# Decode attention in two layers on one core: layer 1's softmax in two passes of four heads

## Chip, cores and metric

One core of one Trainium2 chip. The metric is the device time of one execution in microseconds; lower is better. Times shown here are of the kernel before the change.

## The reference, cut to what matters

Four blocks run one after the other on x (8 sequences of one token, 448 features): attention A, MLP B, then the same A and the same B again. The second pass over A reads the same caches and weights.

```
def _A_ref(x, k_cache, v_cache, wq, wo):
    W = min(4096, max(256, Sk // 4))              # 1024 of 4096 positions
    q = (x @ wq).reshape(B, Sq, 16, 256)          # 16 query heads on 8 KV heads
    k, v = the last W positions of the caches, each KV head used twice
    p = softmax(einsum("bhqd,bhkd->bhqk", q, k) * 256 ** -0.5)
    return einsum("bhqk,bhkd->bhqd", p, v).reshape(B, Sq, 4096) @ wo
def _B_ref(x, w1, w2):
    return silu(x @ w1) @ w2                      # 448 -> 1792 -> 448
x = x + _A_ref(layernorm(x), ...); x = x + _B_ref(layernorm(x), ...)      # layer 1
x = x + _A_ref(layernorm(x), ...); x = x + _B_ref(layernorm(x), ...)      # layer 2
```

All arrays are bfloat16. The window of K and of V is 4 MB for each sequence, 64 MB in all, and the weights are some 12 MB; each of them is read from HBM once.

## The kernel before

**Loads.** A slot holds 1 MB: two KV heads' window of K, or of V. A batch (one sequence) has four K loads and four V loads, in the order K0 to K3, V0 to V3. There are 15 slots in a ring, so load n goes into the place of load n - 15. Since both layers use the same K and V, a K slot is free only when layer 2's scores of its batch are done, and a V slot when layer 2's products are. All these loads stand in the queue of SyncE in their order (`load_kv`, L511) and wait there for the slot.

**One batch.** VectorE turns K in its slot by 32 x 32 blocks (`transposes`, L655; in the names KW for the whole half slot, 1024 wide, KT for 512 wide). TensorE makes the scores (`scores`, L672), named S*layer*.*half*: half 0 is KV heads 0 to 3 from K0 and K1, half 1 heads 4 to 7 from K2 and K3. Half 0 writes 32 rows of each 32-row group, half 1 then writes the first 16 of them, so that one bank of 128 x 256 holds all heads. `softmax` then goes over that bank: maximum on VectorE (L687, max), scaling on ScalarE (L692, mq), a matmul that spreads it (L695, mx), a reduction (L698, mb), the exponential on ScalarE (L699, exp), a permuting matmul (L701, perm), a transpose on VectorE (L703, turn), the sums (L705) and their reciprocal (L708, rl). `products` multiplies with V (L715, PV0 for layer 1, PV1 for layer 2), one V slot at a time. For layer 1 the last V slot's products are separate (`products_late`, L726, in `late`), 256 wide. `o_turn` evicts (L739), turns the output into columns with matmuls (L743) and copies them (L747); `wo_rows` multiplies with wo (L768, wo0 for the first 24 rows and wo7 for the 8 rows of the last V slot). `fold` evicts (L774) and adds the row into x as columns (L544, L547).

`chain` is what follows in the same batch: x masked (L779, xb1), statistics (L785, L788, L790 on GpSimd), w1 in halves (L559) with a turn on VectorE each (L564), tanh (L812) and product (L814), w2 (L826), a second fold, xb2 (L779), statistics, the queries of layer 2 in halves (L841, wq0 and wq1; turns L846; products L847, qm0 and qm1; L854, qx0 and qx1; copies on ScalarE, L858, qbd0 and qbd1). Then come layer 2's scores (S1.0 and S1.1), its softmax and its products.

The queries of layer 1 for all batches are made at the start; `q_blocks1` spreads those of one batch over `qbd[0]` on GpSimd (L641). For the last batch layer 2 has a softmax of its own in two parts; layer 2's MLP runs once for batches 0 to 6 (`final_rows`) and once for batch 7 (`final_last`). `warm` issues matmuls with zero weights (L795, fill) into waits.

**Staging.** In the program order, `chain(b)` and layer 2's attention of batch b stand beside layer 1's attention of batch b + 1:

```
    for b in range(NB):
        chain(b)
        if b < LAST:
            q_blocks1(b + 1)
            attend1(b + 1, 0)
```

This order only makes the dependencies. The order in which each engine really issues its work is written out by hand in `ORDER`, a list of task numbers for TensorE, VectorE, ScalarE and GpSimd; `emit` puts a semaphore wait before a task where another engine's result is needed. Each engine is in order, so a task that waits holds up all that stands behind it on its engine.

**Room.** `qbd[0]` holds layer 1's queries of the current batch: half 0 in columns 16 to 271, half 1 in 272 to 527. `e_sb[0]` and `pT_sb[0]` (exponentials and their transpose) are the same two pieces: `PT[0] = QB(0, 0)`, `EK[0] = QB(0, 1)`.

Of the kernel before, what the change touches and what calls it, by code (L numbers as in the profile page):

```python
# [36 lines left out]
    "dve":  # L37
# [14 lines left out]
    "act":  # L52
# [8 lines left out]
    "pool":  # L61
        "0 1 86 123 124 231 261 262 248 388 357 387 374 522 492 523 509 648 647 617 634 772 773 742 759 867 897 898 "
        "884 1023 1022 992 1009 1110 1127 1154 1217",
}

# [158 lines left out]
def bass_interleave_layers__sliding_block_cached__dense_activation_silu__decode_kernel(  # L224
# [18 lines left out]
    R = 15  # L243
    NP = HKV // 2
    WIDE = (0, 1)
    LATE = 2
    SLOT = 4096
    WARM = (8, 12, 5, 4, 4, 4, 4, 4, 3)
    XC = 5
# [66 lines left out]
    def bk(i):  # L316
        return [("bank", i)]
# [694 lines left out]
    def values1(b):  # L1012
# [9 lines left out]
        for j in range(NP - 1):  # L1022
            products(b, 0, j, OB[0])
# [93 lines left out]
```

## Time and profile before

| what | value |
|---|---|
| three runs | 238.09, 238.39, 242.27 us; median 238.39 |
| the profiled execution | 236.37 us, of which 234.6 us span from the first to the last instruction |
| mean granted TensorE clock | 0.992 |
| PE busy | 175.4 us (75%) |
| DVE busy | 156.9 us (67%), of it K transposes (L655) 79.6 |
| ACT busy | 70.7 us (30%) |
| POOL busy | 22.7 us (10%) |
| moved by DMA | 78.22 MB, mean 333 GB/s |
| chain that ended last | PE 34%, DMA 28%, DVE 25%, ACT 6% |

PE is TensorE's matmuls, DVE is VectorE, ACT ScalarE, POOL GpSimd. A share of busy time is an average over stretches with different limits, so the stretches have to be read one by one. "L655" is line 655 of the kernel before. The chain is followed back from the last instruction to what released it each time.

### The profile page before, as it was taken

The numbers are of one execution on the slowest core, as the hardware profiler recorded it, in microseconds if no ns is written. First come the engines' busy times: TensorE is split into PE (matmuls) and PEld (weight loads), VectorE is DVE, ScalarE is ACT, GpSimd is POOL, SyncE is SP. The second block draws the span as 40 slices with busy tenths as digits, with TensorE's granted clock in tenths as the row PEclk, the third lists the DMA queues.
The fourth block names the chain that finished last, engine by engine and source line by source line (L and its number), as shares of the span: only waits on it lengthen the run. The fifth ranks groups of instructions, "written<-read, shape, count | busy, mean of one in ns | idle before, by whom it ended". The sixth has DMA issues, their size and how long they took to land.

```text
span 234.6 us, 8630 instructions
## 1 busy us (share of the span) xinstructions
PE 175.4 (75%) x3885; PEld 99.1 (42%) x3885; DVE 156.9 (67%) x389; ACT 70.7 (30%) x219; POOL 22.7 (10%) x41
## 2 busy tenths in 40 slices
PE   0021554498878998879859888889898879899994
PEld 0011431134454465356426544455455436554652
DVE  6329899987965794598379739865893588304623
ACT  2000190622222412341333143232422422253332
POOL 1000220002001100120021011000200200001020
PEclk9999999999999999999999999999999979999999
DMA  6999999999999998997999799989987997500000
GB/s 176 422 423 407 380 381 420 412 426 419 418 419 423 395 401 334 426 423 291 383 422 422 292 418 422 419 321 415 423 362 295 419 420 312 183 3 3 3 3 4
DMA packets 13610, 78.22 MB, mean 333 GB/s; under 512 B 1271, under 2 KB 4294, under 8 KB 5126
## 3 DMA queue, kind: packets, MB, share of 16 engines
q1 hardware_dynamic: 13414, 77.32, 81.6%
q8 instruction: 30, 0.49, 0.8%
q10 hardware_dynamic: 160, 0.36, 0.5%
q14 instruction: 6, 0.05, 0.1%
HBM read 77.67 MB, written 0.01 MB: 331 GB/s over the span
## 4 chain that ended last, share of the span: by engine, by line
PE 34%; DMA 28%; DVE 25%; ACT 6%; SPq 2%; issue 2%; POOL 1%; DVEq 0%; ACTq 0%
DMA slot<-in_A_k_cache_dram 28%; DVE slot L655 13%; PE bank L672 9%; DVE slot L482 4%; PE bank L854 4%; PE bank L715 3%; PE pair L841 3%; PE pair L768 3%; PE bank L841 3%; ACT qbd L858 2%; PE pair L826 1%; ACT ot L774 1%; PE bank L785 1%; DVE bank L687 1%; PE pair L544 1%
## 5 line engine op out<-in xcount | busy, mean ns | idle before, releaser
L655 DVE STREAM_TRANSPOSE slot<-slot 128x512 uint32<-128x512 uint32 (+1 forms) x96 | 79.6, 865 | 18.1 <-DMA slot<-in_A_k_cache_dram 17.5
L672 PE MATMUL bank<-slot,qbd 128*32 128x256 bf16 (+1 forms) x1024 | 39.4, 288 | 6.6 <-ACT qbd L858 2.6
L672 PEld LDWEIGHTS bank<-slot,qbd 128*32 128x32 bf16 (+1 forms) x1024 | 26.8, 94 | 15.5 <-ACT qbd L858 5.6
L715 PE MATMUL bank<-slot,qbd 128*24 128x512 bf16 (+3 forms) x416 | 30.6, 394 | 1.1 <-DVE qbd L703 1.0
L795 PE MATMUL bank<-wq_sb,cols 128*1 128x512 bf16 x192 | 19.5, 420 | 10.1 <-DMA wq_sb<-in_A_wq_dram 10.1
L790 POOL TENSOR_TENSOR fcols<-fcols 128x1 f32<-128x1 f32 x17 | 9.4, 552 | 108.0 <-ACT fcols L788 81.8
L739 ACT ACTIVATE ot<-bank,q1s 128x512 bf16<-128x512 f32 (+1 forms) x16 | 10.8, 672 | 26.2 <-DVE q1s L708 10.8
L768 PE MATMUL pair<-wo_sb,q1s 128*1 128x449 bf16 x288 | 15.8, 353 | 0.3 <-ACT q1s L747 0.3
L641 POOL TENSOR_TENSOR qbd<-q1s,fcols 128x256 bf16<-128x256 bf16 x16 | 9.6, 612 | 65.8 <-PE bank L743 39.9
L858 ACT ACTIVATE qbd<-bank 128x256 bf16<-128x256 f32 x16 | 6.1, 383 | 29.7 <-PE bank L854 29.7
L687 DVE CUSTOM_DVE_ANT_1 bank<-bank,fcols 128x256 f32<-128x256 f32 x17 | 7.3, 432 | 10.2 <-PE bank L672 9.4
L715 PEld LDWEIGHTS bank<-slot,qbd 128*24 128x24 bf16 (+3 forms) x416 | 9.5, 93 | 9.6 <-issue 2.4
L692 ACT ACTIVATE fcols<-fcols,q1s 128x16 f32<-128x16 f32 x15 | 4.6, 310 | 24.3 <-DVE q1s L687 19.6
L482 DVE TENSOR_REDUCE slot<-wo_sb 128x6 f32<-128x2688 bf16 x4 | 11.7, 2928 | 0.0
L708 DVE RECIPROCAL q1s<-bank 128x1 f32<-128x1 f32 x17 | 2.8, 162 | 12.6 <-PE bank L705 12.6
L703 DVE STREAM_TRANSPOSE qbd<-bank 128x256 bf16<-128x256 bf16 x17 | 7.9, 467 | 4.3 <-PE bank L701 4.3
L490 ACT ACTIVATE slot<-w_sb 128x448 bf16<-128x448 bf16 x6 | 3.5, 576 | 22.9 <-DMA w_sb<-in_B_w_dram 22.8
L779 DVE TENSOR_TENSOR q1s<-pair,fcols 128x5 bf16<-128x5 f32 x17 | 2.5, 145 | 11.2 <-PE pair L547 11.1
L854 PE MATMUL bank<-qbd,band 128*128 128x64 bf16 x64 | 9.8, 286 | 0.2 <-DVE qbd L847 0.2
L785 PE MATMUL bank<-q1s 128*128 128x1 bf16 x68 | 4.3, 167 | 7.4 <-DVE q1s L779 7.4
L795 PEld LDWEIGHTS bank<-wq_sb,cols 128*1 128x1 bf16 x192 | 4.4, 84 | 12.0 <-issue 10.4
L695 PE MATMUL bank<-fcols,quad 128*32 128x8 f32 x136 | 4.3, 188 | 6.3 <-ACT fcols L692 6.0
(165 smaller groups left out, 265.4 us busy)
## 6 DMA issues: line engine op xcount, KB each, us to landing
slot<-in_A_k_cache_dram SPq DMA_DIRECT2D x32, 1024.0 KB, 10.9
slot<-in_A_v_cache_dram SPq DMA_DIRECT2D x31, 1024.0 KB, 10.8
wo_sb<-in_A_wo_dram SPq DMA_DIRECT2D x4, 896.0 KB, 15.2
wq_sb<-in_A_wq_dram SPq DMA_DIRECT2D x3, 1024.0 KB, 7.9
w_sb<-in_B_w_dram SPq DMA_DIRECT2D x1, 1568.0 KB, 21.8
w_sb<-in_B_w_dram SPq DMA_DIRECT2D x1, 1344.0 KB, 19.3
slot<-in_A_v_cache_dram SPq DMA_DIRECT2D x2, 512.0 KB, 4.8
wq_sb<-in_A_wq_dram ACTq DMA_DIRECT2D x1, 256.0 KB, 3.5
```

Of the source, the lines that this page charges most:

```text
L482: dve(lambda e, rows=rows, s=s: e.tensor_reduce(s, rows[:, :, R0:M1].rearrange("p c (a n) -> p c a n", a=2), AX.X, ALU.add, negate=True), ...
L641: pool(lambda e, k2=k2: e.tensor_tensor(qdata(0, k2), q1s[:, b, 64 * k2:64 * k2 + 64].rearrange("p (n r) -> p n r", r=2).unsqueeze(3) .bro ...
L655: dve(lambda e, v=v: e.transpose(v, v), keys, keys, 0.15 + (i1 - i0) * 512 / 950, b, ("KW%d" if i1 - i0 > 1 else "KT%d") % (2 * j + h))
L672: fns.append(lambda e, w=w, j=j, kv=kv, cb=cb, par=par: e.matmul(sc[32 * j:32 * j + up_to, 0:256], w, kv, start=(cb == 0 and par == 0), st ...
L687: dve(lambda e: e.tensor_tensor_reduce(x.rearrange("p (c h) -> p c h", h=2), x.rearrange("p (c h) -> p c h", h=2), parity.unsqueeze(1).bro ...
L715: pe([lambda e, t=t, h=h: e.matmul(bank[ob][32 * t:32 * t + m, :], pT_sb[L][:, 64 * t + 32 * h:64 * t + 32 * h + m], v[:, 2048 * h + 512 * ...
L739: act(lambda e: e.activation(o_t, src[1], ACTF.Copy, scale=sm[b][:, 4 * L + 3:4 * L + 4]), bk(src[0]) + [("sm", b, L, 3)], okey, 0.62, b, ...
L768: fns.append(lambda e, i=i, w=w, c0=c0: e.matmul(bank[XB][32 * (i % 4):32 * (i % 4) + 1, c0:c0 + D + 1], oT[:, oT_col(i):oT_col(i) + 1], w ...
L795: pe([lambda e, i=i: e.matmul(bank[OB[0]][32 * i:32 * i + 1, :], zero_b, wq_sb[:, 512 * i:512 * i + 512], start=True, stop=True, tile_posi ...
L841: pe([lambda e, j=j, c=c, qh=qh, k2=k2, h=h, n=n: e.matmul(qh[32 * j:32 * j + 1, :], xbt[b][:, xcol(c, k2):xcol(c, k2) + 1], view(wq_sb[:] ...
L854: pe([lambda e, qs=qs, k2=k2, q=q: e.matmul(qs[:, q:256:4], band[:, 96 - 32 * q:224 - 32 * q], view(qm[k2], 0, [(32, 2), (1, 8), (8, 4)]), ...
L858: act(lambda e, qs=qs, k2=k2: e.activation(qbd[1][:, 16 + 256 * k2:272 + 256 * k2], qs, ACTF.Copy), bk(lb), QB(1, k2) + QM * k2, 0.42, b, ...
```

## The change

Layer 1's softmax runs twice for each batch. The pass g = 0 runs after the first half of the scores (heads 0 to 3) and the pass g = 1 after the second half; each goes over the whole bank of 128 x 256, and only the rows of its own half are used. The exponentials of pass g, and then their transpose, lie where the queries of half g were (`eb = pb`), as do the scaled maxima (`m4`). The pass g = 0 uses layer 1's output bank for its small matmuls, the pass g = 1 the bank used before.

The second half's scores go into the same bank as the first half's, so they now wait until the exponential of pass 0 has read it.

The products of V0 and V1 use pass 0 and stay 512 wide. The products of V2 and V3 use pass 1 and are both made 256 wide in `late` (`LATE` is 4 where it was 2), so wo has 16 rows after the first part (wo0) and 16 after the late part (wo7).

The four lists in `ORDER` are new. TensorE's matmuls are 136 more, nine a batch for the extra pass and eight a batch for the halved products; VectorE gets 32 operations more and ScalarE 16. The loads and their order are as before. In the new lists layer 1's products and output rows mostly stand ahead of layer 2's products, xb1 stands ahead of the transposes of the next batch's second K slot or just behind the first one's, and of the final rows of batches 0 to 6 most stand behind layer 2's scores of batch 7.

```diff
-    LATE = 2
+    LATE = 4
...
-    def softmax(b, L, part=None):
+    def softmax(b, L, part=None, g=0):
 
         sb, n, m = (SC[L], L, L) if part is None else (part[0], part[1], 1 - part[1])
-        lb = bank[LB[n]]
+        eb, ek, pb, pk, m4 = e_sb[m], EK[m], pT_sb[m], PT[m], mq
+        mk = ["mq"]
+        lbi, c = LB[n], 4 * n
+        if L == 0:
+            eb = pb = qbd[0][:, 16 + 256 * g:272 + 256 * g]
+            ek = pk = QB(0, g)
+            m4 = eb[:, 0:32].bitcast(F32)
+            mk, n, c = ek, 2 * g, 8 * g
+            lbi = (OB[0], LB[0])[g]
+        lb, lk = bank[lbi], bk(lbi)
...
     def late(b, oT, key):
-        products_late(b, NP - 1, bank[SC[0]][:, 256:512], bk(SC[0]), 0, "PV7%d")
-        o_turn(b, 0, (SC[0], bank[SC[0]][:, 256:512]), ot7, EK[0], 0, 2 * LATE, oT, [(key, b, 7)], "7")
+        for j in range(NP // 2, NP):
+            products_late(b, j, bank[SC[0]][:, 256:512], bk(SC[0]), e_sb[0], EK[0], "PV%d%%d" % (4 + j))
+        o_turn(b, 0, (SC[0], bank[SC[0]][:, 256:512]), ot7, EK[0], 0, 2 * LATE, oT, [(key, b, 7)], "7", 2)
...
-        for j in range(NP - 1):
+        for j in range(NP // 2):
             products(b, 0, j, OB[0])
...
     attend1(0, 0)
+    softmax(0, 0)
     attend1(0, 1)
-    softmax(0, 0)
+    softmax(0, 0, g=1)
...
             attend1(b + 1, 0)
+            softmax(b + 1, 0)
...
             attend1(b + 1, 1)
-            softmax(b + 1, 0)
+            softmax(b + 1, 0, g=1)
```

In `softmax` the rest is as before with `eb`, `pb`, `m4`, `lb` in place of the fixed buffers. The lists in `ORDER` are left out.

More of the change, by code (lines that the diff above doesn't have):

```diff
@@ L676, in scores @@
                bk(sb), 0.0285, b, "S%d.%d" % (layer, k2))
-    def softmax(b, L, part=None):
+    def softmax(b, L, part=None, g=0):
         sb, n, m = (SC[L], L, L) if part is None else (part[0], part[1], 1 - part[1])
-        lb = bank[LB[n]]
+        eb, ek, pb, pk, m4 = e_sb[m], EK[m], pT_sb[m], PT[m], mq
[8 more added lines that the diff above has]
+        lb, lk = bank[lbi], bk(lbi)
         x = bank[sb][:, 0:256]
         px = lb[:, 256:512]
-        mneg, bias, acc, rlr = (sm[b][:, 4 * n + i:4 * n + i + 1] for i in range(4))
+        mneg, bias, acc, rlr = (sm[b][:, c + i:c + i + 1] for i in range(4))
         K = [("sm", b, n, i) for i in range(5)]
@@ L688, in softmax @@
             x.rearrange("p (c h) -> p c h", h=2), x.rearrange("p (c h) -> p c h", h=2),
-            parity.unsqueeze(1).broadcast_to([P, 128, 2]), 1.0, -3e38, ALU.add, ALU.max, mneg), bk(sb) + ["par"],
+            parity.unsqueeze(1).broadcast_to([P, 128, 2]), 1.0, -3e38, ALU.add, ALU.max, mneg), bk(sb) + ["par"] + (QB(0, 1) if L == 0 and g == 0 else []),
             bk(sb) + [K[0]], 0.41, b, "max%d" % L)
         if part is None:
-            act(lambda e: e.activation(mq, sel16, ACTF.Copy, scale=mneg), [K[0], "sel16"], ["mq"], 0.2, b, "mq%d" % L)
+            act(lambda e: e.activation(m4, sel16, ACTF.Copy, scale=mneg), [K[0], "sel16"], mk, 0.2, b, "mq%d" % L)
@@ L693, in softmax @@
         else:
-            dve(lambda e: e.tensor_scalar(mq, sel16, mneg, None, op0=ALU.mult), [K[0], "sel16"], ["mq"], 0.1, b, "mqd")
-        pe([lambda e, t=t: e.matmul(mx[32 * t:32 * t + 32, :], quad[:], mq[:, t // 2 * 8:t // 2 * 8 + 8], start=True,
+            dve(lambda e: e.tensor_scalar(m4, sel16, mneg, None, op0=ALU.mult), [K[0], "sel16"], mk, 0.1, b, "mqd")
+        pe([lambda e, t=t: e.matmul(mx[32 * t:32 * t + 32, :], quad[:], m4[:, t // 2 * 8:t // 2 * 8 + 8], start=True,
                                     stop=True, tile_position=(0, 32 * t), skip_group_check=True) for t in range(4)],
-           ["mq", "quad"], bk(LB[n]), 0.06, b, "mx%d" % L)
@@ L698, in softmax @@
-        dve(lambda e: e.tensor_reduce(bias, mx, AX.X, ALU.max, negate=True), bk(LB[n]), [K[1]], 0.15, b, "mb%d" % L)
-        act(lambda e: e.activation(e_sb[m], x, ACTF.Exp, bias=bias, scale=1.0, accum_out=acc),
-            bk(sb) + [K[1]], EK[m] + [K[2]], 0.6, b, "exp%d" % L)
-        pe(lambda e: e.matmul(px, perm[:], e_sb[m], start=True, stop=True),
-           EK[m] + PERM + QM * m, bk(LB[n]), 0.13, b, "perm%d" % L)
-        dve(lambda e: e.transpose(view(pT_sb[m], 0, [(64, 4), (1, 2), (2, 32)]), px.bitcast(BF16)[:, 1:512:2]),
-            bk(LB[n]), PT[m], 0.44, b, "turn%d" % L)
+           mk + ["quad"], lk, 0.06, b, "mx%d" % L)
@@ new lines, in softmax @@
+        dve(lambda e: e.tensor_reduce(bias, mx, AX.X, ALU.max, negate=True), lk, [K[1]], 0.15, b, "mb%d" % L)
+        act(lambda e: e.activation(eb, x, ACTF.Exp, bias=bias, scale=1.0, accum_out=acc),
+            bk(sb) + [K[1]], ek + [K[2]], 0.6, b, "exp%d" % L)
+        pe(lambda e: e.matmul(px, perm[:], eb, start=True, stop=True), ek + PERM + QM * (m and L), lk, 0.13, b, "perm%d" % L)
+        dve(lambda e: e.transpose(view(pb, 0, [(64, 4), (1, 2), (2, 32)]), px.bitcast(BF16)[:, 1:512:2]), lk, pk, 0.44, b,
+            "turn%d" % L)
@@ L705, in softmax @@
         pe([lambda e, t=t: e.matmul(lr[32 * t:32 * t + 32, :], lsel[:], acc, start=True, stop=True,
                                     tile_position=(0, 32 * t), skip_group_check=True) for t in range(4)],
-           [K[2], "lsel"], bk(LB[n]), 0.05, b, "l%d" % L)
-        dve(lambda e: e.reciprocal(rlr, lr), bk(LB[n]), [K[3]], 0.15, b, "rl%d" % L)
+           [K[2], "lsel"], lk, 0.05, b, "l%d" % L)
+        dve(lambda e: e.reciprocal(rlr, lr), lk, [K[3]], 0.15, b, "rl%d" % L)
     def products(b, L, j, ob):
@@ L719, in products, with products_late @@
                slot_key(slot_of[b, "v", j], h) + PT[L], bk(ob), 0.055, b, "PV%d" % L)
-    def products_late(b, j, o, keys, n, name):
+    def products_late(b, j, o, keys, pt, pk, name):
         v = slots[slot_of[b, "v", j]]
@@ L730, in products_late, with o_turn @@
                 for a in range(2) for t in range(4)],
-               slot_key(slot_of[b, "v", j], h) + PT[n], keys, 0.028, b, name % h if "%" in name else name)
+               slot_key(slot_of[b, "v", j], h) + pk, keys, 0.028, b, name % h if "%" in name else name)
     def late(b, oT, key):
-        products_late(b, NP - 1, bank[SC[0]][:, 256:512], bk(SC[0]), 0, "PV7%d")
-        o_turn(b, 0, (SC[0], bank[SC[0]][:, 256:512]), ot7, EK[0], 0, 2 * LATE, oT, [(key, b, 7)], "7")
-    def o_turn(b, L, src, o_t, okey, c0, c1, dst, keys, name):
-        act(lambda e: e.activation(o_t, src[1], ACTF.Copy, scale=sm[b][:, 4 * L + 3:4 * L + 4]),
-            bk(src[0]) + [("sm", b, L, 3)], okey, 0.62, b, "oev" + name)
+        for j in range(NP // 2, NP):
+            products_late(b, j, bank[SC[0]][:, 256:512], bk(SC[0]), e_sb[0], EK[0], "PV%d%%d" % (4 + j))
+        o_turn(b, 0, (SC[0], bank[SC[0]][:, 256:512]), ot7, EK[0], 0, 2 * LATE, oT, [(key, b, 7)], "7", 2)
+    def o_turn(b, L, src, o_t, okey, c0, c1, dst, keys, name, n=None):
+        n = L if n is None else n
+        act(lambda e: e.activation(o_t, src[1], ACTF.Copy, scale=sm[b][:, 4 * n + 3:4 * n + 4]),
+            bk(src[0]) + [("sm", b, n, 3)], okey, 0.62, b, "oev" + name)
         nz = o_t.shape[-1] // DH
@@ L1054, in values2 @@
             for j in range(2 * k2, 2 * k2 + 2):
-                products_late(b, j, bank[ob][:, 0:256], bk(ob), k2, "PVL")
+                products_late(b, j, bank[ob][:, 0:256], bk(ob), pT_sb[k2], PT[k2], "PVL")
             o_turn(b, 1 - k2, (ob, bank[ob][:, 0:256]), slots[s][:, 512:768] if k2 else ot[:, 0:256],
```

6 lines of the change are left out of this document (3 added, 3 removed), and 91 rows, old and new, of the table ORDER.

## The prediction

> **What bounds the kernel now.** I read the page's slices first, then the queue's waits, then the stretch around one batch, then the chain, then the timeline of the steps that the change doubles. Columns in the slices: 40 slices of 5.87 us.
>
> ```profile
> PE   0021554498878998879859888889898879899994
> DVE  6329899987965794598379739865893588304623
> DMA  6999999999999998997999799989987997500000
> GB/s 176 422 423 407 380 381 420 412 426 419 418 419 423 395 401 334 426 423 291 383 422 422 292 418 422 419 321 415 423 362 295 419 420 312 183 3 3 3 3 4
> ```
>
> Transfers run at 420 GB/s, with a dip about every 22 us from slice 15 on, and end at 205.7 us; then 29 us of pure computing follow. A 1 MB cache load lands every 2.49 us when the queue is full, so eight loads, one batch, take 19.9 us. The dips cost 0.5 to 2 us each, 11 us over all loads up to the last 1 MB. Who makes the queue wait (us in total, times, longest):
>
> ```profile
> SPq L511 <- PE bank L672: 55.6, 11, 12.5
> SPq L511 <- PE bank L715: 36.5, 14, 4.4
> DVE slot L655 <- DMA slot<-in_A_k_cache_dram: 17.5, 9, 7.6
> ```
>
> The load queue waits for layer 2's scores (L672), which free the K slots; VectorE in turn waits for K. So there is one loop per batch: scores of layer 2, softmaxes, products with V, output rows, MLP, queries, scores of layer 2. One turn of it, in windows (busy us of PE, PEld, DVE, ACT, POOL; clock; DMA share; GB/s):
>
> ```profile
> 172.00:174.00 2.00, 2.00 (x32) 0.66 (x25) 1.64 (x4) 0.23 (x1) 0.00 (x0) 1.00 1.03 422
> 174.00:176.00 2.00, 2.00 (x51) 1.48 (x51) 2.00 (x4) 0.54 (x2) 0.00 (x0) 1.00 0.61 246
> 176.00:178.00 2.00, 2.00 (x76) 1.69 (x67) 0.68 (x4) 0.31 (x1) 0.00 (x0) 1.00 0.21 74
> 178.00:180.00 2.00, 1.25 (x26) 0.43 (x17) 1.02 (x5) 1.32 (x5) 0.00 (x0) 1.00 0.96 393
> ```
>
> At 176 the loads have run dry, and at 178 to 180 TensorE idles too: both softmaxes run there one behind the other. The chain shows the second bad place, the wait for K:
>
> ```profile
> 177.25 10.03 DMA slot<-in_A_k_cache_dram
> 187.31 1.25 DVE slot L655
> 188.55 0.06 DVE q1s L779
> ```
>
> VectorE's in-order queue has two K transposes (L655) ahead of the MLP's first step (L779): that step ran at 188.6 although its input, the fold of layer 1 (L547), was ready at 186.7.
>
> I call T the end of the first query matmuls of layer 2 (L854, qx0). T falls at 63.2, 85.4, 107.7, 130.2, 151.6, 173.8, 196.9 and 217.6. From T to the next fold took, in the five middle laps, 13.5, 13.5, 13.4, 13.7 and 12.9 us; from the fold to the next T 8.7, 9.1, 7.9, 8.5 and 10.3. Mean lap 22.3.
>
> **What one more pass costs.** Each batch's layer 1 gets a second softmax over the same 128 partitions; rows of the present pass:
>
> ```profile
> 177.90 0.43 DVE L687 CUSTOM_DVE_ANT_1 bank<-bank,fcols 128x256 f32<-128x256 f32 x1 [0.45 <-PE bank L672]
> 178.25 0.14 DVE L687 DVE_READ_ACCUMULATOR2_ANT q1s<- 128x1 f32 x1
> 179.10 0.17 DVE L698 TENSOR_REDUCE q1s<-bank 128x1 f32<-128x8 f32 x1 [0.69 <-PE bank L695]
> 180.25 0.47 DVE L703 STREAM_TRANSPOSE qbd<-bank 128x256 bf16<-128x256 bf16 x1 [0.22 <-PE bank L701]
> ```
>
> With the reciprocal (L708, 0.16) that is 1.37 us of VectorE a batch, 11 us over eight batches. ScalarE gets 0.31 + 0.45 + 0.19 = 0.95, TensorE 0.25 + 0.28 + 0.21 = 0.74 (L695, L701, L705). The halved products (16 of 0.028 for 8 of 0.055), and the output rows (16 + 16 for 24 + 8), cost nothing by the row rate. Placed out of T's way this work hides under waits: TensorE idles 0.75 us of the window 178 to 180, VectorE 1.32 us of 176 to 178. If that cover is gone it costs its own length.
>
> Two queues are touched by the shared room. GpSimd's new queries (L641, 2 x 0.61) can go in only when the exponentials that now lie there are used; for the second half that is the output turn (L743), which it waits for today too (39.9 us of idle time). Nothing, while layer 1's next scores come 3 us later. SyncE's loads into V slots follow layer 2's products, which now start behind layer 1's: first slot free at T + 9.3 to 9.9, where it was T + 7.0 (180.8) to T + 9.9 (161.5). K's third load lands 13.75 us after layer 2's scores, T + 15.3, and a load issued into an idle queue landed 5.0 us after its issue, so until about T + 12.8 the queue doesn't run dry: 3 us of margin, nothing.
>
> **What it moves, one lap in full.** I follow batch 3's layer 2 and batch 4's layer 1 through the new order, T = 0, each step with its duration in this trace, ends in us. Layer 2's first scores 1.6 (0.41 for L858, then 32 L672). The new first pass (max already done before T): L695 0.35; two K transposes and the reduction on VectorE 0.75; exponential 1.4, just in time for layer 1's second scores, which now overwrite that bank. They and layer 2's second scores end at 3.9 and 4.6 (VectorE: one transpose, qT1 0.7, qm1 0.3, so L858's second copy at 3.3). Second pass: max 4.45, scaling 4.8, L695 5.1, reduction behind layer 2's max 5.35, exponential behind layer 2's scaling 6.2, L701 6.5, turn 7.0. Meanwhile TensorE does the first products. Products of V2 and V3 end at 7.9 and 9.2; eviction 9.7, turn 10.05, copy 10.3, 16 output rows (24 L768 took 1.31 us) 11.4, two product groups 11.9, L774 and fold 12.4. The same sum for the order before gives 13.55, and the trace 13.4; so the method is good to 0.2 us, and this lap wins 1.0.
>
> The other middle laps by the same steps: 12.35, 14.0, 13.9, 12.65, against 13.5, 13.5, 13.7, 12.9. Two gain nothing. In one the first pass's reduction stands behind two transposes and qT1, so its exponential ends at 3.3 and layer 1's second scores wait; in the other these scores come behind layer 2's (5.3), and the turn ends at 8.5. Sum: -1.7.
>
> Fold to T: the wait for K before L779 goes, since at most K's first slot stands ahead of it; but more K transposes stand ahead of the second L779 (xb2), and layer 2's products now fall here, where fills stood. One lap, batch 4, from the fold: L779 0.2, a K transpose ends 1.45, w1 (L559, 32 in 0.6) at 1.1, its turns (L564) 1.85 and 2.2, tanh and product (L812, L814) 2.8, w2 (L826) 3.5, L774 4.15, fold 4.55, second L779 behind three transposes 5.5, statistics and the queries' L841 (1.05 + 0.9, between waits) 7.8, L854 8.4. In the order of the laps 8.6, 8.5, 8.4, 8.65, 8.6, against 44.5 in all: -1.75.
>
> Start: VectorE is busy from 24 to 52 either way; w1's turns go ahead of K's, one pass more comes in. S1.0 of batch 0 between -0.3 and +0.6: +0.3. First lap: S1.1 of batch 0 comes behind batch 1's first pass (its max has seven transposes and turns ahead of it), fold at 78.8 where it was 77.65; then the MLP's two turns each stand behind a 1.2 us transpose, T at 87.5 to 88 where it was 85.4. Bounds +0.5 and +2.5; nearer to neither: +1.5. Last lap: the last load's second half lands 6.5 us after layer 2's scores (199.2 to 205.7) as now; the 24 rows that followed it have mostly gone ahead: -1.2. Tail, from S1.0 of batch 7 to the end, 14.75 us: the final rows of batches 0 to 6 are put later. Ahead of the second L701 now stand eight matmuls of L904 (22 took 1.14: 0.4) and more; ahead of batch 7's output turns the w18 matmuls of L559 (0.6) and the statistics; ahead of ScalarE's last tanh the eviction of L927's rows, and L927 itself (0.75) now follows batch 7's w1 instead of running before it: 0.4 + 0.6 + 0.75 + 0.65 = 2.4 if all show, 0 if none: +1.2.
>
> Sum: +0.3 + 1.5 - 1.7 - 1.75 - 1.2 + 1.2 = -1.65. The profiled run took 236.37 (span 234.6 and 1.8 around it), 2.0 below the median 238.39; on the median this gives 236.7. Each lap's error, 0.5, and the two bounds above make its own range 233 to 241. A measurement here tells about 2% from no change: 233.6 and 243.2.
>
> **Rivals.** *The loop falls to the pace of the loads.* If the two poor laps do as well as the good ones and fold to T takes the 7.9 seen once, laps take 20.2 (floor 19.9): 5 x (22.3 - 20.2) = -10.5, with the other terms +1.8: 229.7. For it: the dips, 11 us; against it: the poor laps are in the order itself.
>
> *VectorE's queue becomes the bound* (slower). It is full from 172 to 176 (1.64 and 2.00 of 2), where the first pass is put, ahead of transposes that layer 1's second scores need. If the scores, not the exponential, end last there, all 1.37 show in each of the five middle laps and the last: +6.85 for -1.7, +0.2 for -1.2. Sum 0.3 + 1.5 + 6.85 - 1.75 + 0.2 + 1.2 = +8.3: 246.7. It decides once K's last transpose ends later than 1.6 us after T; in my lap it ends at 1.4, so the margin is thin, but VectorE has 2 to 3 us of waiting before the next K lands that takes it up.
>
> *TensorE's clock* (the granted share stands third from the end):
>
> ```profile
> 190.00:192.00 2.00, 2.00 (x32) 1.02 (x32) 1.75 (x6) 0.53 (x3) 0.00 (x0) 0.53 0.96 401
> 192.00:194.00 2.00, 1.26 (x22) 0.38 (x15) 0.88 (x4) 0.64 (x1) 0.00 (x0) 0.62 1.06 442
> ```
>
> Here w2 ended 1.8 us after its input (190.9 to 192.8), in other laps 0.8. My 8.6 for that lap leaves this 1.0 out. Fills are moved; if it came in each of seven laps: -1.65 + 7 x 1.0 = +5.35, 243.7. Against it: layer 2's products now stand in those gaps. [...]
>
> *It doesn't do what it says:* the fourth V load ends last in every lap (5.0 us after its issue at T + 1.6, so 6.6) and the -1.7 and -1.2 are not gained: +1.25, 239.6. Against: V3's products come at 8 to 10.
>
> **Chances.** Forecast 0.53, pace of the loads 0.22, VectorE 0.14, clock 0.06, no effect 0.05. Faster by over 2%: the pace case and a tenth of the forecast, 0.26; slower: most of VectorE's and half of the clock's, 0.17; within: 0.57. Likeliest 236.7; range 231 to 243.5.
>
> **What would show it.** Right: laps alternating between about 21 and 22.5; L779 no longer behind a K load; dips in GB/s a little shallower; first T later than 85.4 by 1 to 2.5; a tail of 15 to 17 us; VectorE's busy time up by 11 us. Wrong: laps near 20 with flat GB/s (first rival); VectorE with no idle time and L672 waiting for L655 or L699 in all laps (second); granted clocks below 0.7 in many windows (third); first V products waiting on V's load (fourth).

## The result and the profile after

The changed kernel takes 235.81 us (median of 20 runs, 233.56 to 237.23), the kernel before 238.24 in runs beside it: a ratio of 0.9909, interval 0.9882 to 0.9937. Measured a second time it was 0.9888 (0.9830 to 0.9945). The ratios leave out executions that took over 1.5% longer than the fastest of their kernel. So it is faster by about 1%, 2.2 us by the ratio. The forecast was 236.7 in a range of 231 to 243.5.

One caution for reading the traces. The profiled execution of before (span 234.6) lies 1.9 us under its median, the first one of after (span 235.0) 1.0 above its own, so these two spans don't show the gain. The second measurement left another profile of the same changed kernel (span 232.0, also about 1 us under its median). "First" and "second" below are these two profiles of the changed kernel.

The slices of the first profile, in the same columns as before (5.87 us each):

```profile
PE   0052044787699888888897989998999789999995
DVE  6508799996994797489549755994996389434443
DMA  6999999999989997999999879999998989600000
GB/s 177 410 424 408 379 380 412 418 428 420 417 315 389 424 417 275 418 424 409 301 390 425 342 261 423 417 383 418 424 418 326 421 329 421 259 3 3 3 4 4
```

The dips of the loads are still there in most laps, to 261 to 329 GB/s: the loop has not come down to the pace of the loads. The waits, of SyncE's queue and then of VectorE for K (us in total, times, longest):

```profile
SPq L514 <- PE bank L675: 40.4, 6, 12.0
...
SPq L514 <- PE bank L726: 14.2, 8, 4.3
```

```profile
DVE slot L658 <- DMA slot<-in_A_k_cache_dram: 14.2, 9, 2.8
```

The load queue waits 40 us for layer 2's scores where it waited 56, but other waits have taken the place: all its waits for slots between 60 and 206 us come to 127 us before, 125 in the first profile and 134 in the second. Nor does VectorE wait less for K. The longest wait before, 7.6 us, ended at 16.0 us, in the start, where the first load is on its way. From 60 us on, before and then in the first profile:

```profile
DVE slot L655 <- DMA slot<-in_A_k_cache_dram: 9.1, 7, 2.4
DVE slot L658 <- DMA slot<-in_A_k_cache_dram: 13.3, 8, 2.8
```

So the loads don't come sooner; what has changed is what stands behind them. The stretch shown of before, 172 to 180, in the second profile, where T falls at 173.29 (before: 173.75):

```profile
172.00:174.00 2.00, 1.71 (x34) 0.81 (x30) 1.97 (x7) 0.41 (x2) 0.00 (x0) 1.00 1.07 438
174.00:176.00 2.00, 2.00 (x69) 1.62 (x58) 1.57 (x4) 0.54 (x2) 0.00 (x0) 1.00 0.56 221
176.00:178.00 2.00, 1.77 (x56) 1.38 (x56) 1.00 (x6) 1.03 (x4) 0.00 (x0) 1.00 0.81 295
178.00:180.00 2.00, 2.00 (x58) 0.87 (x49) 1.17 (x5) 0.92 (x4) 0.00 (x0) 1.00 1.03 410
```

TensorE works 2.00 us in 178 to 180 where it had 1.25, and the loads are running again at 176 (295 GB/s, before 74). What the second pass cost, in the groups of the first profile (line, shape, count, busy us and mean ns):

```profile
L714 DVE STREAM_TRANSPOSE qbd<-bank 128x256 bf16<-128x256 bf16 x25 | 11.9, 474 | 7.5 <-PE bank L713 7.3
L699 DVE CUSTOM_DVE_ANT_1 bank<-bank,fcols 128x256 f32<-128x256 f32 x25 | 10.6, 423 | 5.2 <-PE bank L675 4.9
L719 DVE RECIPROCAL q1s<-bank 128x1 f32<-128x1 f32 x25 | 3.9, 157 | 4.3 <-PE bank L716 3.5 <-PE bank L707 0.8
L710 DVE TENSOR_REDUCE q1s<-bank 128x1 f32<-128x8 f32 x25 | 3.9, 155 | 5.9 <-PE bank L707 5.8
```

Each is there 25 times, before 17. And the step that before ended 1.4 to 2.0 us behind the fold in batches 2, 3 and 6, with K transposes ahead of it, now in batch 3 of the first profile (VectorE's timeline; start, length, what; the fold ended at 122.87):

```profile
121.71 1.20 DVE L658 STREAM_TRANSPOSE slot<-slot 128x1024 uint32<-128x1024 uint32 x1
122.84 0.13 DVE L719 RECIPROCAL q1s<-bank 128x1 f32<-128x1 f32 x1
123.66 1.24 DVE L658 STREAM_TRANSPOSE slot<-slot 128x1024 uint32<-128x1024 uint32 x1 [0.69 <-DMA slot<-in_A_k_cache_dram]
124.83 0.12 DVE L792 TENSOR_TENSOR q1s<-pair,fcols 128x5 bf16<-128x5 f32 x1
```

There xb1 (now L792) still ran 2.0 us late, behind a K transpose that waited for its load. In batches 0, 1, 2, 6 and 7 it ran right after the fold.

By the terms of the prediction, us against the profile of before:

| term | predicted | first profile | second profile |
|---|---|---|---|
| start and first lap (T of batch 0's layer 2, then of batch 1's) | +1.8 | +2.9 | +2.7 |
| five middle laps, T of batches 1 to 5 to the next fold | -1.7 | -1.0 | -2.0 |
| batches 2 to 6, fold to T | -1.75 | -0.2 | -2.5 |
| last lap | -1.2 | -2.2 | -1.8 |
| tail | +1.2 | +1.0 | +1.0 |
| sum | -1.65 | +0.4 | -2.6 |

The sums are the differences of the spans. The two profiles of one kernel differ by 3.0 us, most of it in one place, batch 3's fold to T: 11.06 us in the first and 8.43 in the second. What happens there is taken up with the last experiment. Both the profile of before (at 190, in batch 6's fold to T) and the first one (at 126, in batch 3's) have one stretch of 3.4 us at half clock in the loop; the second profile has none.

### The profile page after: what moved, and what is told of

The parts are those of the page before. It is cut to its first block, busy times and chain, and to the rows that moved or that the text cites. A ratio compares the mean times of both kernels' runs of the same rounds, so it can differ in the third digit from the quotient of the medians.

```text
span 235.0 us, 9083 instructions
## 1 busy us (share of the span) xinstructions
PE 178.5 (76%) x4085; PEld 100.5 (43%) x4085; DVE 164.1 (70%) x429; ACT 77.8 (33%) x243; POOL 22.7 (10%) x41
## 4 chain that ended last, share of the span: by engine, by line
PE 41%; DVE 26%; DMA 19%; ACT 7%; issue 4%; SPq 2%; POOL 0%; ACTq 0%; DVEq 0%
DMA slot<-in_A_k_cache_dram 19%; DVE slot L658 14%; PE bank L675 10%; PE bank L726 4%; PE pair L781 4%; PE bank L808 3%; PE bank L737 3%; PE bank L867 3%; DVE slot L485 2%; PE pair L854 2%; DVE bank L699 2%; ACT ot L787 2%; PE bank L854 2%; PE bank L713 1%; PE pair L839 1%
## 5 line engine op out<-in xcount | busy, mean ns | idle before, releaser
L675 PE MATMUL bank<-slot,qbd 128*32 128x256 bf16 (+1 forms) x1024 | 39.5, 290 | 9.9 <-POOL qbd L644 6.0
L675 PEld LDWEIGHTS bank<-slot,qbd 128*32 128x32 bf16 (+1 forms) x1024 | 24.9, 94 | 19.3 <-DVE fcols L418 6.2
L781 PE MATMUL pair<-wo_sb,q1s 128*1 128x449 bf16 x288 | 17.6, 353 | 0.8 <-issue 0.5
L714 DVE STREAM_TRANSPOSE qbd<-bank 128x256 bf16<-128x256 bf16 x25 | 11.9, 474 | 7.5 <-PE bank L713 7.3
L711 ACT ACTIVATE qbd<-bank,q1s 128x256 bf16<-128x256 f32 x25 | 11.8, 472 | 11.7 <-DVE q1s L710 11.2
L737 PE MATMUL bank<-slot,qbd 128*7 128x256 bf16 (+3 forms) x320 | 13.6, 276 | 1.9 <-issue 1.9
L699 DVE CUSTOM_DVE_ANT_1 bank<-bank,fcols 128x256 f32<-128x256 f32 x25 | 10.6, 423 | 5.2 <-PE bank L675 4.9
L752 ACT ACTIVATE ot<-bank,q1s 128x512 bf16<-128x512 f32 (+1 forms) x16 | 10.8, 673 | 6.1 <-PE bank L726 5.4
L713 PE MATMUL bank<-qbd,perm 128*128 128x256 bf16 x25 | 7.3, 292 | 6.2 <-ACT qbd L711 5.7
L485 DVE TENSOR_REDUCE slot<-wo_sb 128x6 f32<-128x2688 bf16 x4 | 11.7, 2932 | 0.0
L839 PE MATMUL pair<-w_sb,q1s 128*1 128x449 bf16 x112 | 8.5, 380 | 1.8 <-DVE w_sb L488 1.0
L704 ACT ACTIVATE qbd<-fcols,q1s 128x16 f32<-128x16 f32 x16 | 4.9, 308 | 14.4 <-DVE q1s L699 9.5
L854 PE MATMUL pair<-wq_sb,q1s 128*1 128x256 bf16 x256 | 9.1, 276 | 0.6 <-ACT q1s L845 0.6
## 6 DMA issues: line engine op xcount, KB each, us to landing
wo_sb<-in_A_wo_dram SPq DMA_DIRECT2D x4, 896.0 KB, 14.5
```

Of the source, the lines that this page charges most:

```text
L485: dve(lambda e, rows=rows, s=s: e.tensor_reduce(s, rows[:, :, R0:M1].rearrange("p c (a n) -> p c a n", a=2), AX.X, ALU.add, negate=True), ...
L675: fns.append(lambda e, w=w, j=j, kv=kv, cb=cb, par=par: e.matmul(sc[32 * j:32 * j + up_to, 0:256], w, kv, start=(cb == 0 and par == 0), st ...
L699: dve(lambda e: e.tensor_tensor_reduce(x.rearrange("p (c h) -> p c h", h=2), x.rearrange("p (c h) -> p c h", h=2), parity.unsqueeze(1).bro ...
L711: act(lambda e: e.activation(eb, x, ACTF.Exp, bias=bias, scale=1.0, accum_out=acc), bk(sb) + [K[1]], ek + [K[2]], 0.6, b, "exp%d" % L)
L714: dve(lambda e: e.transpose(view(pb, 0, [(64, 4), (1, 2), (2, 32)]), px.bitcast(BF16)[:, 1:512:2]), lk, pk, 0.44, b, "turn%d" % L)
L737: pe([lambda e, t=t, a=a, h=h: e.matmul(o[32 * t:32 * t + m, :], pt[:, 64 * t + 32 * h + a:64 * t + 32 * h + a + m], v[:, 2048 * h + 512 * ...
```

## Experiments

Differences are taken between ratios to the kernel before: that of the changed kernel is 0.9909, and 0.01 is 2.4 us. By the intervals they are good to 1.0 to 1.8 us. Moves are written as in `_move('dve', ['550'], before='513')`: take task 550 out of VectorE's list and put it before task 513. Theories: A, the two passes and the new orders both matter and the pass hides under waits; O, the order of the MLP step is all the gain; V, VectorE's queue sets the pace.

**e1: before, with the MLP step first.** In the kernel before, xb1 goes ahead of the next batch's second K slot in batches 2 to 6, on VectorE alone.

```diff
+_move('dve', ['489'], before='527')    # xb1 of batch 2 ahead of KW2, KW3 of batch 3
+_move('dve', ['526'], after='500')     # KW2 behind hTb
+...                                    # the same in batches 3 to 6
```

> The kernel before with one thing of the new order: in batches 2 to 6 VectorE's first MLP step (L779) stands ahead of the second K slot's transposes (L655), with one of these behind it and the other behind the MLP's product. No second pass. Theory A (the passes and the order both matter): the three waits of 1.1, 2.0 and 1.7 us ahead of L785 in the profile before go, but the transposes then run later and give a part back: -1 to -2 us, about 0.994 of the time before. Theory O (the order of this step is all of the change's gain, and the second pass brings nothing): -2.4 us or more, 0.990 or below. Theory V (VectorE's queue as a whole sets the pace): no change, 1.000.

Measured: 245.44 us, ratio 1.0348 (1.0272 to 1.0424) to before, +8.3 us. All three theories missed. The waits from fold to xb1 did go (0.20 to 0.26 us in batches 2 to 5, 0.90 in batch 6), but TensorE's list still had the next batch's first scores ahead of w2, and these need both K slots. TensorE's weight loads in batch 2, then its windows (last three columns: granted clock, DMA share, GB/s):

```profile
99.88 0.36 PEld L579 LDWEIGHTS bank<-w_sb,q1s 128*1 128x1 bf16 x16
102.84 0.56 PEld L692 LDWEIGHTS bank<-slot,qbd 128*32 128x32 bf16 x16 [2.60 <-DVE slot L675]
```

```profile
104.00:108.00 4.00, 3.74 (x56) 2.02 (x57) 1.24 (x3) 1.04 (x4) 0.00 (x0) 0.50 1.01 422
108.00:112.00 4.00, 3.95 (x52) 1.68 (x44) 2.47 (x6) 0.14 (x2) 0.55 (x1) 0.50 0.34 139
```

After w1 (L579) TensorE stood 2.6 us before the scores (L692) that wait for the moved transposes (L675), and it ran at half clock from 102 to 112 us (granted 0.50). A step moved on one engine alone turned its wait into a worse one on the next. So the order of VectorE's MLP step by itself is no gain, and O falls in its plain form.

**e2: after, with the MLP step late again.** In batches 2, 4 and 6 the next batch's second K slot goes back to where it was: its first half (KW2) ahead of xb1, its second half (KW3) ahead of w1's turns.

```diff
+_move('dve', ['550'], before='513')    # KW2 of batch 3 ahead of xb1 of batch 2
+_move('dve', ['551'], before='518')    # KW3 ahead of w1Ta
+...                                    # the same in batches 4 and 6
```

> The changed kernel with this order undone in batches 2, 4 and 6: both transposes of the second K slot stand around L792 as before the change (one ahead of it, one between it and the w1 turns). Theory A: three waits of 1 to 2 us come back, partly hidden: +1.5 to +4 us on 235.8. Theory O: at least half of the gain is lost, +1.2 us or more. Theory V: no change.

Measured: 238.26 us, ratio 1.0038 (0.9998 to 1.0079): +3.1 against the changed kernel. A and O hold, V (0) falls. Fold to xb1 took 1.22, 0.94 and 1.21 us in these batches, 0.20 to 0.67 in the first profile. TensorE's wait for xb1 ahead of the statistics, in the first profile of the changed kernel and then in e2 (in total, times, longest; before: 9.9, 13, 2.1):

```profile
PEld bank L798 <- DVE q1s L792: 5.7, 12, 2.1
```

```profile
PEld bank L814 <- DVE q1s L808: 8.8, 13, 1.9
```

**e3: after, with the first pass doubled.** VectorE's four operations of pass 0 are done twice, 1.35 us a batch, 10.8 us in all by the groups.

```diff
+        def dve(fn, reads, writes, dur, row, name):
+            for again in (False, True) if L == 0 and g == 0 else (False,):
+                add("dve", fn, ..., again=again)     # the second one directly behind the first
```

> The changed kernel with VectorE's four operations of the first pass (max, reduction, turn, reciprocal) each done twice, 1.37 us more of VectorE in each of eight batches, 11 us in all. Theory A (the pass hides under waits): 0 to +3 us. Theory V (VectorE's queue sets the pace): +8 to +11 us.

Measured: 242.12 us, ratio 1.0216 (1.0157 to 1.0276): +7.3, or 0.68 us for each us added. A's "0 to +3" missed, and V's "+8 to +11" lies just above. Most of what is added here isn't hidden.

**e4: after, with layer 1's products late.** The products of V0 and V1, which the first pass makes possible early, go directly ahead of those of V2.

```diff
+_move('pe', ['331', '332', '333', '334'], before='345')   # PV0 of batch 1 ahead of PV60
+...                                                       # the same in batches 2 to 7
```

> The changed kernel with the products of V0 and V1 of layer 1 (four groups a batch, 0.9 us) put behind the second pass, directly ahead of the products of V2 (in batch 7 ahead of the fill there), so that the first pass is there but nothing uses it early. Theory A (the early products fill the second pass's wait): +0.5 to +0.9 us a lap, +3 to +6 us. Theory O: 0 to +1 us.

Measured: 240.11 us, ratio 1.0104 (1.0036 to 1.0171): +4.6. A holds, O (0 to +1) falls. T to fold, batches 2 to 6, took 13.5, 14.5, 12.7, 15.8 and 13.6 us, 70.0 in all, where the two profiles of the changed kernel have 65.9 and 65.0. So what the two passes gain, they gain by the products taken early in the wait for the second pass.

The next two ask whether e3 showed VectorE's time or the latency of the pass's own chain. Theory P: time counts where the first pass stands; C: only the pass's own chain counts; Q: VectorE's time counts anywhere.

**e5 and e6: idle reductions.** Three reductions into an unused column in each batch, 0.49 to 0.50 us each.

```diff
+    def idle(b):
+        add("dve", lambda e: e.tensor_reduce(fcols[:, 47:48], wq_sb[:, 0:342], AX.X, ALU.add), ...)
# e5: one behind each of max, mb and turn of the first pass
+        if L == 0 and g == 0:
+            idle(b)
# e6: three behind rl of the second pass
+        for _ in range(3 * (L == 0 and g == 1)):
+            idle(b)
```

> The changed kernel; in each batch VectorE gets three reductions that nobody reads (about 0.46 us each, 1.37 us in all, as much as the doubled operations of e3), one behind each of the first pass's maximum, bias and turn. Unlike in e3 nothing of the pass waits for them; only what is queued behind them on VectorE does. Theory P (time on VectorE's queue shows where the first pass stands, ahead of the query's turn and the second slot's transposes): +5 to +9 us against the changed kernel. Theory C (only the first pass's own chain counts, so that the doubling of e3 showed as latency): 0 to +2.5. Theory Q (VectorE's time sets the pace wherever it is added): +5 to +9.

> The changed kernel with the same three idle reductions in each batch, all behind the reciprocal of the second pass (rl0 of heads 4 to 7), where VectorE waits for the fold next. Theory P: 0 to +2 us against the changed kernel. Theory C: 0 to +2. Theory Q: +5 to +9.

Measured: e5 239.01 us, ratio 1.0096 (1.0061 to 1.0131), +4.4; e6 238.30, ratio 1.0019 (0.9983 to 1.0054), +2.6. The reductions took 11.7 and 12.1 us, so 0.38 and 0.22 us for each us added. No theory's number is met. The order of the three prices, 0.68 in the chain, 0.38 on the queue beside it, 0.22 behind the second pass, is that of P; e5 and e6 lie 1.8 us apart, give or take 1.2. Q's +5 to +9 for e6 falls, and C's 0 to +2.5 for e5; P has the order right and both sizes a little off.

**e11: after, without the first pass's maximum.** The other direction. Left out in each batch are the first pass's maximum, scaling, spreading matmul and reduction; the exponential takes a constant bias.

```diff
+        skip = L == 0 and g == 0
+                if skip and name[:-1] in ("max", "mq", "mx", "mb"):
+                    add("none", fn, gone=True)
+        if skip:
+            bias = mask5[:, 0:1]
```

> The changed kernel without the maximum of the first pass: its four instructions (maximum and bias on VectorE, 0.72 us a batch, 5.7 us in all, and the small copy and matmuls between them) are left out in each batch and the exponential takes a constant bias. If the pass's VectorE time costs what e3, e5 and e6 showed for added time (0.24 to 0.67 us per us): -1.4 to -3.8 us against the changed kernel. If the pass as it stands hides under waits and only more than it shows: 0 to -1.

Measured: 235.05 us, ratio 0.9888 (0.9834 to 0.9943), beside 0.9888 for the changed kernel in e9: 0.0, give or take 1.9. VectorE's part of this is 5.7 us by the groups. The page of e11, against 164.1 or 164.2 us of VectorE's busy time in the two profiles of the changed kernel (records overlap a little, so the busy time falls by less):

```profile
PE 174.8 (75%) x4021; PEld 98.8 (43%) x4021; DVE 161.1 (69%) x405; ACT 74.7 (32%) x235; POOL 22.7 (10%) x41
```

At e3's price this would have given -3.9, which the interval excludes; at e6's, -1.3, which it doesn't. So the pass's maximum, as it stands, costs less for each us than what e3 put on top. Whether all of it hides, or it costs up to 1.9 us, these runs can't tell.

**e7: after, with batch 0's layer 2 queries first.** In the start, two K transposes (1.8 us) stand on VectorE ahead of the turn of batch 0's queries; they go behind it, and batch 1's first scores behind batch 0's.

```diff
+_move('pe', ['275', '276', '277', '278'], after='291')   # S0.0 of batch 1 behind S1.0 of batch 0
+_move('pe', ['281'], after='297')                        # mx0 behind S1.1
+_move('dve', ['272', '312'], after='261')                # KW1, KT5 behind qm0
+_move('dve', ['266'], after='265')                       # qm1 right behind qT1
```

> The changed kernel, one place alone: in batch 0, VectorE turns the query products before the first two K transposes of the second slot, and TensorE takes batch 0's layer 2 scores before batch 1's first layer 1 scores. Theory P (the 1.8 us that the two transposes stand ahead of the query's turn in the start are lost for good, as the comparison of the traces has the start and first lap 2.9 us longer): -1.2 to -2.2 us against the changed kernel. Rival (the first lap is bound by batch 1's K transposes and takes the time back): -0.4 to +0.8.

Measured: 237.34 us, ratio 1.0010 (0.9973 to 1.0046): +2.4, which nobody expected. Layer 2's first scores ended at 65.76 (first profile 67.37), so the 1.6 us were won. But the next T came at 89.41 (88.35): the first pass of batch 1 was now late, TensorE was busy for 1.81 of 4.00 us from 66 to 70, and the granted clock was 0.58 and 0.56 in 70 to 72 and 72 to 74. In this order, what the start won was lost again in the lap behind it.

**e8: after, with the tail's order changed.**

```diff
+_move('pe', ['1208'], after='1207')    # last quarter of wo8 behind the third
+_move('pe', ['1219'], after='1216')    # first half of w18 behind stat8
```

> The changed kernel, the tail alone: the final rows' last quarter of wo8 stands directly behind the third and the first half of w18 behind stat8, not ahead of it. If the tail's extra 1 us comes from this order of TensorE's work: -0.4 to -0.9 us against the changed kernel. If the tail is bound by layer 2's chain of the last batch (exponential, turn, products, fold): -0.2 to +0.3.

Measured: 235.92 us, ratio 0.9947 (0.9913 to 0.9980): +0.9, give or take 1.0. The stretch from S1.0 of batch 7 to the end took 15.89 us, 15.71 in the first profile. The extra microsecond of the tail doesn't come from these matmuls; where it comes from stays open.

**e9: the changed kernel once more**, and **e10: the MLP step first in batches 3 and 5 too**, with the lesson of e1: the next batch's first scores go behind w2.

```diff
+_move('dve', ['646'], before='683')                # xb1 of batch 3 ahead of KW2
+_move('dve', ['653', '651'], before='684')         # w1Tb, w1Ta ahead of KW3
+_move('pe', ['685', '686', '687'], after='659')    # S0.0 of batch 4 behind w2b
+...                                                # the like in batch 5, hTa and hTb ahead of KW3 too
```

> The changed kernel as it is, once more, as the measure for the runs beside it: ratio to the kernel before 0.988 to 0.994 by the first measurement.

> The changed kernel; in batches 3 and 5, where VectorE still has the next batch's third K transpose (KW2) ahead of xb1, xb1 comes first, the third and fourth transposes stand behind xb1 and behind the MLP's turns, and on TensorE the next batch's first scores stand behind w2, so that nothing of the MLP step queues behind them (which e1 lacked). Theory P (what VectorE does between the fold and xb1 is on the path): the waits of 2.1 and 0.7 us from fold to xb1 go, and -1.5 to -3 us against the changed kernel. Rival (the next batch's first scores and first pass, now later, become the path, as in e1): 0 to +2.

Measured: e9 as told above. e10 237.27 us, ratio 1.0036 (0.9994 to 1.0078): +3.5 against e9. P falls; the rival has the sign right, with a mechanism of its own. (The interval of that difference is 1.7 to either side.) VectorE in batch 3, fold at 122.77, and TensorE's windows:

```profile
122.80 0.17 DVE L808 TENSOR_TENSOR q1s<-pair,fcols 128x5 bf16<-128x5 f32 x1 [0.33 <-PE pair L566]
123.95 1.25 DVE L674 STREAM_TRANSPOSE slot<-slot 128x1024 uint32<-128x1024 uint32 x1 [0.98 <-DMA slot<-in_A_k_cache_dram]
125.12 0.35 DVE L583 STREAM_TRANSPOSE bank<-bank 128x192 f32<-128x192 f32 x1
125.38 0.42 DVE L583 STREAM_TRANSPOSE pair<-pair 128x256 f32<-128x256 f32 x1
125.71 1.80 DVE L674 STREAM_TRANSPOSE slot<-slot 128x1024 uint32<-128x1024 uint32 x2
127.43 0.13 DVE L843 SCALAR_TENSOR_TENSOR q1s<-q1s,pair 128x8 bf16<-128x8 f32 x1
```

```profile
124.00:128.00 4.00, 1.15 (x35) 0.52 (x27) 4.00 (x8) 0.78 (x3) 0.41 (x1) 1.00 1.01 422
128.00:132.00 4.00, 4.00 (x71) 2.44 (x67) 2.43 (x6) 0.94 (x3) 0.00 (x0) 0.57 1.02 430
```

xb1 is early, but the K transpose that was ahead of it now waits 0.98 us for its load one step further on, ahead of w1's turns (L583), and more transposes stand ahead of the product for w2 (L843). TensorE has nothing to do for 2.85 of the 4.00 us from 124 to 128, and the granted clock is 0.57 in the 4 us after that. The wait for K was moved, not taken away.

**e12: fills in the gap of batch 3.** In the first profile TensorE idled 1.62 us between fold and statistics in batch 3, and its clock then fell:

```profile
124.00:126.00 2.00, 0.99 (x36) 0.77 (x36) 2.00 (x3) 0.70 (x2) 0.36 (x1) 1.00 1.03 430
126.00:128.00 2.00, 1.98 (x40) 0.94 (x36) 2.00 (x8) 0.57 (x3) 0.20 (x1) 0.55 1.01 422
128.00:130.00 2.00, 2.00 (x30) 0.72 (x22) 1.33 (x3) 0.15 (x1) 0.00 (x0) 0.60 0.98 414
```

```diff
+_move('pe', ['616', '617', '618'], before='647')   # three fills ahead of stat1 of batch 3
```

> The changed kernel; in batch 3 TensorE's three fill matmul groups (the next lines of work that only keep it busy, 0.66 us in all) stand directly ahead of stat1, where the profile of the changed kernel has TensorE idle for 1.62 us behind the fold, not behind oT1 and w2. In the profiles so far each stretch of half clock began 2 to 4 us after an idle gap of TensorE of 1.48 us or more, and none followed a gap of 1.40 us or less. Theory I (the idle gap brings the half clock): the gap falls under 1.4 us, no half clock between 120 and 135 us, and 0 to -1.5 us against the changed kernel in the median, for only part of its runs have the gap that long. Rival (the half clock comes without regard to the gap, or the fills, now ahead of stat1, delay it): 0 to +0.7, and half clock can show there still.

Measured: 235.75 us, ratio 0.9925 (0.9871 to 0.9978): no change that can be measured. In its profile xb1 ran 1.98 us behind the fold, nearly as late as in the first profile (2.10), the gap was 0.85 us, and the clock stayed:

```profile
126.00:128.00 2.00, 1.37 (x30) 0.42 (x22) 1.97 (x6) 0.81 (x3) 0.00 (x0) 1.00 0.98 414
128.00:130.00 2.00, 1.84 (x55) 1.36 (x59) 1.93 (x6) 0.90 (x5) 0.55 (x1) 1.00 1.04 438
```

Fold to T was 9.46 us there, 11.06 in the first profile: 1.6 less with the same lateness of xb1. Other profiles agree: in batch 3, fold to T took 11.24 and 10.49 us in e3 and e6, which have the half clock there (granted 0.50 in 128 to 130 and in 126 to 128), and 9.15 to 9.81 in e2, e7, e8 and e11, which don't, with xb1 1.7 to 2.1 us late in all six. In one execution, then, the half clock costs some 1 to 2 us, an estimate from these times; in the median over 12 runs the change doesn't show, and the changed kernel rarely has the half clock anyway (below). None of the versions tried beats the changed kernel.

## Why the prediction was right, and where not

**The sum** (-1.65; measured -2.2 by the ratio). The terms were near, and that their errors cancel (start and first lap +1.0, last lap -0.8) is luck. They are also all taken against one profile of before, 1.9 us under its median and with one stretch of half clock in it.

**What the sum left out: the clock.** Each run has its mean granted clock on record. In the runs below it is either 0.997 or more, or 0.993 or less; one stretch of 3.4 us at half clock in 235 us makes 0.993 (1 - 0.5 x 3.4 / 235). These are the runs that the ratios count: of before those beside the experiments, of the changed kernel those of both measurements.

| kernel | runs | full clock: runs, mean us | half clock somewhere: runs, mean us |
|---|---|---|---|
| before | 56 | 14, 235.60 | 42, 237.15 |
| changed | 24 | 20, 235.45 | 4, 236.58 |
| e2, MLP step late again | 10 | 4, 237.51 | 6, 238.04 |
| e4, products late | 4 | 3, 238.80 | 1, 240.23 |
| e7, batch 0's queries first | 10 | 5, 236.15 | 5, 237.89 |

At full clock the two kernels take the same time (0.15 us apart, give or take 0.6), and the -1.65 isn't there. What differs is how often TensorE falls to half clock: in 42 of 56 runs before, in 4 of 24 after. By this reading most of the 1% is clock that is kept. e2 points to TensorE's shorter waits: with the MLP step late again, its wait for xb1 is 8.8 us (5.7 in the first profile), and 6 of 10 runs have half clock somewhere. e2 and e4 cost time at full clock too, so the early step and the early products do gain, but at full clock about as much as the second pass, the start and the tail cost. This is a comparison of runs, not an experiment: runs of before at full clock may be those whose waits happened to be short, and no run takes the half clock out of the kernel before with nothing else changed. So the cause of the 1% stays in part open. The prediction knew the clock only as a rival that makes the changed kernel slower, though about 1.0 us of its -1.75 came from leaving out the half clock of batch 6's lap.

**T to fold, -1.7.** Right in kind and size: -1.0 and -2.0. Lap by lap the forecast was 12.35, 14.0, 12.4, 13.9 and 12.65; the second profile has 12.3, 13.3, 12.3, 13.9 and 13.1. e4 shows the mechanism: with the products of V0 and V1 late, 4 to 5 us of T to fold come back.

**"This work hides under waits."** Shown in part, for the pass as it stands: e11 tests its maximum, half of its VectorE time, and leaves anything from nothing to 1.9 us. The prediction called the margin thin, and e3, e5 and e6 show that there is none: each microsecond that was added shows with 0.2 to 0.7. The second rival (VectorE's queue becomes the bound) was the right thing to fear, though it overstates it: it had +8.3 against before with the pass once, and e3, with the pass's VectorE work twice, came to +5.1.

**VectorE's busy time up by 11 us.** The groups of the pass rose by 10.6 us as worked out, the page's busy time by 7.2. On the timeline records overlap a little at their ends (121.71 + 1.20 runs past 122.84 by 0.07), and the busy time counts that once; over the 40 added operations 0.07 makes 2.8 of the 3.4 us between the two figures.

**Fold to T, -1.75.** The step "the wait for K before L779 goes, since at most K's first slot stands ahead of it" is wrong in batches 3 and 5: by VectorE's list the first half of the second slot (KW2) still stands ahead of xb1 there. In batches 3 to 5 xb1 ended 2.10, 0.67 and 0.45 us behind the fold in the first profile and 0.93, 0.44 and 0.76 in the second, where 0.20 is no wait. The term came out at -2.5 in the second profile all the same, and by the prediction's own estimate about 1 us of that is the half clock at 190 to 194, which the trace of before had and its 8.6 for this lap did without. In the first profile the half clock fell into this term on the other side, and it was -0.2.

**Start +0.3, first lap +1.5.** Together too small by 1. The start was the mis-sized term: layer 2's first scores of batch 0 ended 2.3 us later in the first profile and 2.9 in the second, and from there to the next T it took 0.6 longer in the first and 0.2 less in the second. The prediction had counted VectorE as full either way; it hadn't counted that KW1 and KT5 of batch 1 now stand ahead of the turn of batch 0's queries. e7 shows that this isn't a plain loss either.

**Last lap, -1.2.** Too small: -2.2 and -1.8, nearly all of it between T of batch 6 and the fold of batch 7. With the products late (e4) 1.2 to 1.6 us of it come back; the output rows that went ahead were not tested. **Tail, +1.2:** +1.0, but not by the order of TensorE's work that the prediction listed first (e8).

**The rivals.** The pace of the loads: laps of 18.5 to 24.4 and dips to 261 GB/s say no. TensorE's clock: as a loss in each lap, no; by the runs' granted clocks it was the other way round, a loss of the kernel before, as told above. "It doesn't do what it says": no, TensorE waited for a V load once from 60 us on, 0.3 us in the first profile and 0.7 in the second.

## What to carry to other kernels

Work that is doubled to start something earlier can cost nothing only as long as it fits the wait that it is put into: price it by adding to it and by taking from it, for the two answers can differ (here 0.68 us for each us added to the pass, and 0 to 0.33 for each us taken from it). Moving a step forward on one in-order engine helps only if the other engines' lists and the load behind it move along; otherwise its wait appears one step further on, as in e1 (+8.3 us) and e10 (+3.5). When the profiled runs lie apart from their medians by as much as the effect, take a second profile of the same kernel before explaining a difference, and set the runs' granted clocks beside their times: here they show a gain that a sum of waits doesn't.

## What the runs showed of the hardware

**Half clock after short gaps.** From 60 to 224 us, in windows of 2 us, the 14 profiles of this study show nine stretches at half clock: one each in before, the first profile, e3, e6, e7 and e10, and three in e1. They last 3.4 us, in e1 once 10.2: in the first profile (1 - 0.55) / 0.5 x 2 + (1 - 0.60) / 0.5 x 2 = 3.4, in e10 3.4 by the same sum over its 4 us. In before TensorE idled (neither matmul nor weight load) for 1.69 us at 186.96 and had half clock from 190.10, in the first profile for 1.62 us at 123.39 and had half clock from 126.20, so 3.1 and 2.8 us after the gap began. The gaps of 1.10 us at 99.26 in before and of 1.27 at 184.85 in the first profile had no such effect, but neither had the longest of the two profiles in this span, 2.01 us at 121.12 in before. That the gap brings the half clock is borne out by e12 in one profile only.

The 3.41 us just ahead of the half clock, in before and in the first profile (busy 1.71 and 1.77 of 3.41 us):

```profile
186.69:190.10 3.41, 1.71 (x52) 1.16 (x52) 3.36 (x6) 0.94 (x2) 0.55 (x1) 1.00 1.01 418
122.79:126.20 3.41, 1.77 (x51) 0.91 (x52) 2.71 (x6) 0.84 (x2) 0.55 (x1) 1.00 1.01 425
```

Around the gap of 2.01 us, from 121.00 to 124.41 in before, TensorE was busy for less, 1.40 of 3.41 us, and the granted clock stayed at 1.00 up to 190.10; in e1 it was busy for 1.74 of 4.00 us from 196 to 200, and the clock stayed at 1.00 up to 224. What tells these waits from the ones that cost the clock, no run here shows.

**Stops within a group.** In the first profile TensorE idled 1.28 us within the products of V3, up to 186.13, with nothing that the profile shows to wait for ("issue"). Ahead of matmuls of the late products such stops come to 0.7 us, once, in the second profile and to 1.8 us in e2 (three, the longest 1.0). The page of the first profile counts 4085 matmuls and as many weight loads, so nothing points to a hole in the record. What it is, no run here tells.
